# Expert stage: w1 loaded twice with its sums a block ahead, casts queued behind bank copies, first half-pass of w2 by plain products

## The chip, the core and the metric

The kernel runs on one core of a Trainium2 chip. The metric is the device time of one execution in microseconds (us), the median over runs. TensorE (PE) multiplies, VectorE (DVE) and ScalarE (ACT) copy, add and cast, GpSimd (POOL) does elementwise differences, and the DMAs are issued from SyncE's queue (SP).

## The reference, cut to what matters

```python
x = attention(q, k, v)                       # 2 x 8 heads, 576 tokens, 64 wide
x = (silu(x @ w_gate) * (x @ w_val)) @ w_out  # 1152 tokens, 512 wide, 1536 hidden
P = sinkhorn(exp(x @ w_gate2 - max))          # 1152 x 8, eight rounds of row and column scaling
for e in range(8):                            # the stage that is changed
    h = np.maximum(x @ w1[e], 0.0)            # 512 -> 1024
    out += P[:, e:e + 1] * (h @ w2[e])        # 1024 -> 512
```

## The kernel before

Every float32 operand is split into a high part (a rounding cast on ACT, `fp32r`) and a low part (the difference, `sub`, line 70, on DVE), and every product is three matmuls: high by high, high by low, low by high. Attention and the gated layer come first and are not changed; the expert stage (`experts`) starts at 378 us of the profile.

The expert stage goes through 16 passes, `n`: half of an expert's hidden units each (four tiles of 128). A pass has two halves of the tokens, `c`. For each half, `Group` computes the hidden units with w1: seven products `p1` to `p7` instead of eight (Strassen's scheme in Winograd's form), so w1 is needed both plain (`b`, 768 columns) and as differences of its 256-column blocks (`t`, 1024 columns). `Pair` multiplies four 128-token tiles of the first half by w2, again by seven products, so w2 is needed plain (`Q[:, 0:4]`) and as differences (`Q[:, 4:7]` and `T2`). The rest is done by plain products: `tile_product` (line 850), 12 matmuls of 512 columns a tile; in every pass that is the odd tile (`last_tile`) and the four tiles of the second half.

Units are interleaved by `block`: two Groups, or two Pairs, in the order p1, p5 of each, then p6, p2, then p7, p3, then p4. A product accumulates onto a bank that an ACT copy has seeded (`seeded`, line 689: it copies the running sum into a fresh PSUM bank and returns it, named `u`, `y` or `b`), so the next product on that bank waits for the copy. The last p4 of a block is done inside the next block (`late`). PE and POOL keep the written order; the order on ACT, DVE and SP is laid by the scheduler, which fills gaps by its own estimates. Within one engine instructions run strictly in that order.

The weights: `load_raw` (line 97) loads 512 KB of w1 or w2 into one of three buffers `raw`. `prep1` loads a w1 tile once, casts `b` from it (line 115), then lets POOL make the differences in place (`differences`, line 104, four operations on 128x256), then casts `t` from the same buffer (line 120). In every pass these steps stand at p1 of the first Pair. `second_sums` does the same for w2's differences: load, POOL, cast (line 865); `second` loads w2 again and casts it plain. The two w1 tiles and the two w2 tiles of a pass therefore give 16 POOL operations, one after the other, in the Pair block and the Group block behind it.

`behind()` queues what is traced inside it, on ACT, after the last bank copy (`mark[0]`). `emit` scales and adds a product to the output accumulator `acc` on DVE (line 780). `gate` computes P in 14 small steps, between products of the first passes, at the counts in `GSTEPS`.

Of the kernel before, what the change touches and what calls it, by code (L numbers as in the profile page):

```python
# [29 lines left out]
GSTEPS = {10, 16, 45, 54, 58, 78, 83, 88, 107, 112, 117}  # L30
# [30 lines left out]
def fused(ctx, tc, qk, v, rope, wgv, wo, wg2, w1, w2, out):  # L61
# [44 lines left out]
    def prep1(W1, n, u, src):  # L106

        if u not in W1:  # L110
            W1[u] = new_w(), new_w()
        raw = load_raw(src)
        yield
        (bh, bl), (th, tl) = W1[u]
        nc.scalar.copy(out=bh[:, 0:768], in_=raw[:, 0:768])
        sub(bl[:, 0:768], raw[:, 0:768], bh[:, 0:768])
        yield
        differences(raw, (1, 3, 0, 2))
        yield
        nc.scalar.copy(out=th, in_=raw)  # L120
        sub(tl, raw, th)
        yield
# [488 lines left out]
    def w_out(x2, x32, ps, uh, ul, W1):  # L611
# [12 lines left out]
        for d in range(KD):  # L624
            for c in range(NC):
                if d == KD - 1 and c == 0:
                    for _ in prep1(W1, 0, 0, w1[0, :, 0:WU]):
                        pass
# [15 lines left out]
    def experts(x, x32, ep, banks, W1):  # L644
# [22 lines left out]
        def sums(c):  # L667
            s = token_sums(x32, c)
            o = token_halves(c)[2]
            for i in (1, 2, 0, 3):  # L670
                nc.scalar.copy(out=sh[:, i, :, o], in_=s[i])
                sub(sl[:, i, :, o], s[i], sh[:, i, :, o])
# [19 lines left out]
        mark = [None]  # L692
# [77 lines left out]
        def emit(n, t, half, src, w=256):  # L770
            dst = acc[:, t, 256 * half:256 * half + w]
            e = n // 2
            if e == 0:
                if (t, half) not in touched:
                    touched.add((t, half))
# [88 lines left out]
        def cast(hi, lo, src):  # L864
            nc.scalar.copy(out=hi, in_=src)  # L865
            sub(lo, src, hi)

# [51 lines left out]
        def second_sums(n, u):  # L919
            raw = load_raw(source(w2, n, u))  # L920
            yield
            differences(raw, (0, 1, 2, 3))
            yield
            cast(*(y[:, 4:7, u] for y in Q), raw[:, 0:768].rearrange("p (a c) -> p a c", a=3))
            cast(*(y[:, u] for y in T2), raw[:, 768:1024])
            yield

        def second(n, u):
            raw = load_raw(source(w2, n, u))
            yield  # L930
            cast(*(y[:, 0:4, u] for y in Q), raw.rearrange("p (a c) -> p a c", a=4))
            yield
# [102 lines left out]
        def steps(make, n):  # L1035

            if n >= NV:
                return lambda: None
            gens = [make(n, u) for u in range(2)]
            return lambda: [next(y, None) for y in gens]  # L1040

        def first_(n, u):
            return prep1(W1, n, u, source(w1, n, u))

        acc = None
        with tc.manual_schedule(engines={mybir.EngineType.PE, mybir.EngineType.Pool}):
            A, C = Group(0, 0, 0), Group(0, 0, 1)
            A.p1()
            for _ in range(3):
                next(g)  # L1050
            with behind():
                sums(0)
            A.p2()
            C.p1(True)
            for _ in first_(0, 1):
                pass
            step2, step1 = steps(second_sums, 0), steps(second, 0)
            step2()
            step2()
            A.p6()  # L1060
            with behind():
                step2()
# [3 lines left out]
            A.p3()  # L1066
            acc = ep.tile([128, NTT, DM], F32, tag="acc", name="acc")
            Bq = Group(0, 1, 0)
            Bq.p1()
            with behind():  # L1070
                sums(1)
# [3 lines left out]
            step1()  # L1075
            Bq.p2()
            Bq.p7()
            Bq.p3()
            C.again()
            Bq.p4()  # L1080
            for t in token_tasks(0):
                run(t)
            tokens_left(0, 0)

            def held(step):
                def go():
                    with behind():
                        step()
# [106 lines left out]
```

## Time and profile before

| | before |
|---|---|
| median of 3 runs | 1163.57 us (1162.12 to 1164.08) |
| profiled execution, its own time | 1161.39 us |
| its span | 1159.6 us |
| PE busy | 1130.0 us (97%) |
| DVE busy | 858.9 us (74%) |
| ACT busy | 635.8 us (55%) |
| POOL busy | 355.2 us (31%) |
| mean DMA rate | 84 GB/s |

The span is the profile's own clock from its first to its last instruction; the execution's time lies 1.8 us above it. A busy share is an average over the whole span: attention, the gated layer, and the 16 passes of the expert stage, which fill the last two thirds.

### The profile page before, as it was taken

The page shows a single profiled execution, that of the slowest core. Times are in us where ns is not written, and L with a number is a line of the kernel's source. Part 1 is how long each engine was busy: PE and PEld are TensorE (multiplying, and loading weights), DVE is VectorE, ACT ScalarE, POOL GpSimd, SP SyncE. Part 2 cuts the span into 40 slices and gives each one's busy share as a digit, 9 for nine tenths or more (in the row PEclk, how much of TensorE's full clock was granted, in tenths as well). Part 3 has the DMA queues.
Part 4 walks back from the last instruction along what each step waited for, and adds up shares of the span by engine and source line. Part 5 has one row for each costly group of instructions (what it writes and reads, how often), then busy time and mean ns, then how long its engine had stood idle before and what let it go on. Part 6 is the DMA issues. An engine that isn't in the chain of part 4 may idle for free.

```text
span 1159.6 us, 19384 instructions
## 1 busy us (share of the span) xinstructions
PE 1130.0 (97%) x7431; PEld 1042.0 (90%) x7431; DVE 858.9 (74%) x1498; ACT 635.8 (55%) x1323; POOL 355.2 (31%) x360
## 2 busy tenths in 40 slices
PE   9999999999999899999999999999999999999998
PEld 7777789999999788898998989989899898998997
DVE  6777879988752877887767877768677786777864
ACT  4777744444332776465654656546565465564651
POOL 5777210000010450432504415144051350523500
PEclk9999999999999999999999999999999999999999
DMA  5877413322221131211312122122221222212202
GB/s 179 243 204 192 150 40 112 119 88 79 75 68 43 55 107 40 73 56 56 94 52 73 56 71 94 37 73 71 65 85 37 74 73 74 73 38 73 82 11 82
DMA packets 29837, 97.57 MB, mean 84 GB/s; under 512 B 4912, under 2 KB 5424, under 8 KB 28336
## 3 DMA queue, kind: packets, MB, share of 16 engines
q1 hardware_dynamic: 29744, 96.34, 27.1%
q8 instruction: 58, 0.95, 0.3%
q14 instruction: 35, 0.29, 0.1%
HBM read 81.58 MB, written 2.36 MB: 72 GB/s over the span
## 4 chain that ended last, share of the span: by engine, by line
PE 71%; POOL 20%; DVE 5%; issue 3%; ACT 2%; POOLq 0%; DVEq 0%; ACTq 0%
POOL raw L104 20%; PE y L850 19%; PE u L174 5%; PE u L176 4%; PE u L175 4%; PE s L299 4%; PE pv L411 4%; PE t L339 3%; PE po L176 2%; PE po L175 2%; PE po L174 2%; PE pg L174 2%; PE pv L176 2%; PE pg L176 2%; PE pv L174 2%
## 5 line engine op out<-in xcount | busy, mean ns | idle before, releaser
L104 POOL TENSOR_TENSOR raw<-raw 128x256 f32<-128x256 f32 x256 | 263.7, 1037 | 686.0 <-DVE wl L70 639.4
L70 DVE TENSOR_TENSOR hl<-d,hh 128x256 fp32r<-128x256 f32 (+1 forms) x224 | 138.5, 630 | 49.3 <-ACT hh L865 49.2
L865 ACT CAST hh<-d 128x256 fp32r<-128x256 f32 (+1 forms) x224 | 115.0, 527 | 91.5 <-PE y L850 45.1
L174 PE MATMUL u<-sh,wh 128*128 128x288 f32 x384 | 115.2, 300 | 10.8 <-ACT u L689 10.8
L175 PE MATMUL u<-sl,wh 128*128 128x288 f32 x384 | 113.4, 295 | 0.7 <-DVE sl L70 0.7
L176 PE MATMUL u<-sh,wl 128*128 128x288 f32 x384 | 113.3, 295 | 0.0
L70 DVE TENSOR_TENSOR wl<-raw,wh 128x768 fp32r<-128x768 f32 (+1 forms) x64 | 78.6, 1229 | 31.2 <-ACT wh L120 31.2
L850 PE MATMUL y<-qh,hl 128*128 128x512 f32 x256 | 99.7, 389 | 0.0
L850 PE MATMUL y<-qh,hh 128*128 128x512 f32 x256 | 99.6, 389 | 0.0
L850 PE MATMUL y<-ql,hh 128*128 128x512 f32 x256 | 99.6, 389 | 0.0
L699 DVE TENSOR_TENSOR d<-u,d 128x288 f32<-128x288 f32 x128 | 58.0, 456 | 42.2 <-PE u L176 41.2
L174 PEld LDWEIGHTS u<-sh,wh 128*128 128x128 f32 x384 | 72.6, 189 | 14.8 <-ACT u L689 14.8
L70 DVE TENSOR_TENSOR ql<-raw,qh 128x768 fp32r<-128x768 f32 (+1 forms) x64 | 71.9, 1123 | 16.1 <-ACT qh L865 16.0
L780 DVE SCALAR_TENSOR_TENSOR acc<-y,Pm,acc 128x512 f32<-128x512 f32 (+1 forms) x98 | 65.7, 670 | 23.8 <-PE y L850 21.6
L174 PE MATMUL c<-xh,wh 128*128 128x288 f32 x256 | 75.5, 295 | 0.3 <-ACT d L944 0.3
L176 PE MATMUL c<-xh,wl 128*128 128x288 f32 x256 | 75.2, 294 | 0.0
L175 PE MATMUL c<-xl,wh 128*128 128x288 f32 x256 | 75.0, 293 | 0.0
L175 PEld LDWEIGHTS u<-sl,wh 128*128 128x128 f32 x384 | 72.7, 189 | 0.9 <-DVE sl L70 0.9
L176 PEld LDWEIGHTS u<-sh,wl 128*128 128x128 f32 x384 | 72.7, 189 | 0.0
L886 DVE TENSOR_TENSOR d<-d 128x256 f32<-128x256 f32 x128 | 53.4, 419 | 18.2 <-ACT d L702 17.6
L865 ACT CAST qh<-raw 128x768 fp32r<-128x768 f32 (+1 forms) x64 | 60.2, 942 | 7.5 <-POOL raw L104 7.5
L320 ACT ACTIVATE p<-s,ng 128x576 f32<-128x576 f32 x64 | 47.6, 745 | 28.9 <-DVE ng L304 28.4
(225 smaller groups left out, 3439.1 us busy)
## 6 DMA issues: line engine op xcount, KB each, us to landing
raw<-in_w SPq DMA_DIRECT2D x96, 512.0 KB, 3.9
raw<-in_wgv SPq DMA_DIRECT2D x11, 1024.0 KB, 4.9
x<-in_qk SPq DMA_DIRECT2D x14, 576.0 KB, 5.6
raw<-in_wo SPq DMA_DIRECT2D x12, 512.0 KB, 3.7
x<-hl SPq DMA_DIRECT2D x42, 144.0 KB, 3.5
x<-hl SPq DMA_DIRECT2D x14, 288.0 KB, 3.6
v<-in_v SPq DMA_DIRECT2D x8, 320.0 KB, 4.5
out<-acc SPq DMA_DIRECT2D x9, 256.0 KB, 2.0
```

The source lines that it names most:

```text
L70: (eng or nc.vector).tensor_tensor(out=out_, in0=a, in1=hi.bitcast(F32), op=ALU.subtract)
L104: nc.gpsimd.tensor_tensor(out=o, in0=p, in1=q, op=ALU.subtract)
L174: nc.tensor.matmul(ps, wh[wsl], xh[xsl], start=first, stop=False, skip_group_check=onto)
L175: nc.tensor.matmul(ps, wh[wsl], xl[xsl], start=False, stop=False, skip_group_check=onto)
L176: nc.tensor.matmul(ps, wl[wsl], xh[xsl], start=False, stop=last, skip_group_check=onto)
L299: nc.tensor.matmul(ps[:, c, o:o + ks.stop - ks.start], q, k, start=t == 0, stop=t == len(terms) - 1)
L320: nc.scalar.activation(out=pr.rearrange("p (a c) -> p a c", a=2), in_=SC.pop((n, u))[:, :, 0:288], func=AF.Exp, bias=R.pop((n, u)), scale= ...
L699: nc.vector.tensor_tensor(out=out_, in0=a, in1=b, op=ALU.add)
L780: nc.vector.scalar_tensor_tensor(out=dst, in0=src, scalar=Pm[:, t, e:e + 1], in1=dst, op0=ALU.mult, op1=ALU.add)
L850: nc.tensor.matmul(po.rearrange("p (a c) -> p a c", a=2), a, b, start=m == j == 0, stop=m == 3 and j == 2)
L865: nc.scalar.copy(out=hi, in_=src)
L886: nc.vector.tensor_tensor(out=o, in0=a, in1=b, op=op)
```

## The change

- w1 is loaded twice: 768 columns into `R[2]` for the plain cast (`b_load`, `b_cast`), 1024 into `R[0]` or `R[1]` for the differences (`t_load`, `t_cast`). The three buffers are fixed ones now. `t_load` stands in the Group block of the second half, right after the plain w2 cast that frees the buffer, a block ahead of its cast; w2's differences (`s_load`) follow the w1 cast in the Pair block, and are cast in the Group block behind it.
- The casts stand behind the last bank copy on ACT and, on DVE, behind the last addition (`mark[1]`).
- In pass 0 the four tiles of the first half are done by `plain_tile` instead of two Pairs, so pass 0 needs no differences of w2; the first sums of x are made before the first product; `GSTEPS` has other counts.

```diff
-        raw = load_raw(src)
...
-        nc.scalar.copy(out=bh[:, 0:768], in_=raw[:, 0:768])
-        sub(bl[:, 0:768], raw[:, 0:768], bh[:, 0:768])
...
-        differences(raw, (1, 3, 0, 2))
...
-        nc.scalar.copy(out=th, in_=raw)
-        sub(tl, raw, th)
+    def cast(hi, lo, src):
+        nc.scalar.copy(out=hi, in_=src)
+        sub(lo, src, hi)
...
+                    nc.sync.dma_start(out=R[2][:, 0:768], in_=w1[0, :, 0:768])
+                    nc.sync.dma_start(out=R[0], in_=w1[0, :, 0:WU])
+                    cast(*(y[:, 0:768] for y in W1[0][0]), R[2][:, 0:768])
+                    differences(R[0], (1, 3, 0, 2))
...
         def behind():
-            return tc.issue_after(mark[0].ins)
+            with ExitStack() as st:
+                for m in mark:
+                    if m is not None:
+                        st.enter_context(tc.issue_after(m.ins))
+                yield
         def add(out_, a, b):
-            nc.vector.tensor_tensor(out=out_, in0=a, in1=b, op=ALU.add)
+            mark[1] = nc.vector.tensor_tensor(out=out_, in0=a, in1=b, op=ALU.add)
...
+        def b_load(n, u):
+            load(2, w1, n, u, 768)
+        def b_cast(u):
+            cast(*(y[:, 0:768] for y in W1[u][0]), R[2][:, 0:768])
+        def t_load(n, u):
+            load(u, w1, n, u)
+            differences(R[u], (1, 3, 0, 2))
+        def t_cast(u):
+            cast(*W1[u][1], R[u])
+        def s_load(n, u):
+            load(u, w2, n, u)
+            differences(R[u], (0, 1, 2, 3))
+        def s_cast(u):
+            cast(*(y[:, 4:7, u] for y in Q), R[u][:, 0:768].rearrange("p (a c) -> p a c", a=3))
+            cast(*(y[:, u] for y in T2), R[u][:, 768:1024])
+        def q_cast(u, r):
+            cast(*(y[:, 0:4, u] for y in Q), R[r].rearrange("p (a c) -> p a c", a=4))
...
-                block([Pair(w, 0, s) for s in range(2)], merge(plain_tasks(w), {(1, 0): [held(step) if n == 1 else step, step, step]}),
+                if n == 1:
+                    for i in range(2):
+                        for r in range(2):
+                            plain_tile(0, 0, i, r)
...
+                else:
+                    block([Pair(w, 0, s) for s in range(2)], merge(plain_tasks(w), {
+                        (5, 1): [held(b_cast, 1), now(b_load, n + 1, 0)],
+                        (6, 0): [held(t_cast, 0), now(s_load, n, 0)],
+                        (2, 1): [held(t_cast, 1), now(s_load, n, 1)]} if n < NV else {}),
...
-                    block([Group(n, u, 0) for u in range(2)], {(6, 0): [step2]}, behind=BEHIND[1:])
+                    block([Group(n, u, 0) for u in range(2)], {(7, 1): [held(s_cast, 0), now(load, 0, w2, n, 0)]}, behind=BEHIND[1:])
                 last_tile(w)
...
+                    held(s_cast, 1)()
+                    load(1, w2, n, 1)
...
-                    block([Group(n, u, 1) for u in range(2)], {(6, 0): [step]}, behind=BEHIND[1:])
+                    block([Group(n, u, 1) for u in range(2)], {
+                        (1, 0): [held(q_cast, 0, 0)] + [now(t_load, n + 1, 0)] * (not last),
+                        (1, 1): [held(q_cast, 1, 1)] + [now(t_load, n + 1, 1)] * (not last),
+                        (3, 0): [held(b_cast, 0), now(b_load, n + 1, 1)] * (not last)}, behind=BEHIND[1:])
```

The order of ACT in the Pair block of one pass, before (`wh` is w1's high part, `raw` its buffer, `qh` and `xh<-raw` w2's differences, `hh` a cast of hidden units, `y`, `b`, `u2` the bank copies; every pass from the third on repeats it):

```order
L865 CAST hh0_4310<-d_4309 128x2x2x128 [waits PE_49,Activation_49]
L689 COPY y_11144<-x_11137 128x256 [waits PE_49]
L120 CAST wh_4152<-raw_11031 128x1024 [waits Pool_49]
L865 CAST hh1_4312<-d_4309 128x2x2x128 [waits PE_49]
L689 COPY b_11163<-y_11101 128x256 [waits PE_49]
L689 COPY b_11178<-y_11144 128x256 [waits PE_49]
L120 CAST wh_4387<-raw_11033 128x1024 [waits Pool_49]
L865 CAST xh_2317<-raw_11219 128x256 [waits DMAHW0_49,Pool_49]
L689 COPY u2_11230<-c11_11223 128x288 [waits DVE_49,PE_49]
```

And the same place of the changed kernel:

```order
L107 CAST hh0_4315<-d_4314 128x2x2x128 [waits PE_49,Activation_49]
L683 COPY y_11477<-x_11470 128x256 [waits PE_49]
L107 CAST wh_4157<-raw2_4152 128x768 [waits DMAHW3_49]
L107 CAST hh1_4317<-d_4314 128x2x2x128 [waits PE_49]
L683 COPY b_11498<-y_11450 128x256 [waits PE_49]
L107 CAST wh_4155<-raw0_4150 128x1024 [waits DMAHW1_49,Pool_49]
L683 COPY b_11520<-y_11477 128x256 [waits PE_49]
L107 CAST wh_4159<-raw1_4151 128x1024 [waits DMAHW2_49,Pool_49]
L683 COPY u2_11575<-c11_11568 128x288 [waits DVE_49,PE_49]
```

A plain cast of w1 from the third buffer has come in behind the second `y` copy, each 1024-column cast stands behind a `b` copy, and the cast of w2's differences no longer stands ahead of `u2`.

The order of DVE at the same place, before (`wl` is w1's low part, `acc<-b` the addition that reads bank `b`):

```order
L780 SCALAR_TENSOR_TENSOR acc<-z,Pm,acc 128x256 [waits PE_49]
L780 SCALAR_TENSOR_TENSOR acc<-z,Pm,acc 128x256
L70 TENSOR_TENSOR wl<-raw,wh 128x1024 [waits Activation_49]
L780 SCALAR_TENSOR_TENSOR acc<-x,Pm,acc 128x256 [waits PE_49]
L70 TENSOR_TENSOR hl_4313<-d,hh_4312 128x2x2x128 [waits Activation_49]
L780 SCALAR_TENSOR_TENSOR acc<-x,Pm,acc 128x256 [waits PE_49]
L780 SCALAR_TENSOR_TENSOR acc<-b,Pm,acc 128x256 [waits DVE_49,PE_49]
L70 TENSOR_TENSOR wl<-raw,wh 128x1024 [waits Activation_49]
L780 SCALAR_TENSOR_TENSOR acc<-y,Pm,acc 128x256 [waits PE_49]
L780 SCALAR_TENSOR_TENSOR acc<-b,Pm,acc 128x256 [waits DVE_49,PE_49]
```

And now:

```order
L779 SCALAR_TENSOR_TENSOR acc<-z,Pm,acc 128x256 [waits PE_49]
L779 SCALAR_TENSOR_TENSOR acc<-z,Pm,acc 128x256
L70 TENSOR_TENSOR wl<-raw_4152,wh 128x768 [waits DMAHW3_49,Activation_49]
L70 TENSOR_TENSOR hl_4318<-d,hh_4317 128x2x2x128 [waits Activation_49]
L779 SCALAR_TENSOR_TENSOR acc<-x,Pm,acc 128x256 [waits PE_49]
L70 TENSOR_TENSOR wl<-raw_4150,wh 128x1024 [waits DMAHW1_49,Activation_49]
L779 SCALAR_TENSOR_TENSOR acc<-x,Pm,acc 128x256 [waits PE_49]
L779 SCALAR_TENSOR_TENSOR acc<-b,Pm,acc 128x256 [waits DVE_49,PE_49]
L70 TENSOR_TENSOR wl<-raw_4151,wh 128x1024 [waits DMAHW2_49,Activation_49]
L779 SCALAR_TENSOR_TENSOR acc<-y,Pm,acc 128x256 [waits PE_49]
L779 SCALAR_TENSOR_TENSOR acc<-b,Pm,acc 128x256 [waits DVE_49,PE_49]
```

The two 1024-column differences keep their places among the additions, and one of 768 columns comes in ahead of them.

SP's queue for one pass of the changed kernel (before, it was six loads of 128x1024):

```order
L916 DMA raw_4152<-in_w 128x768 [waits DMAHW4_49,DVE_49]
L916 DMA raw_4152<-in_w 128x768 [waits DMAHW3_49,DVE_49]
L916 DMA raw_4150<-in_w 128x1024 [waits DMAHW1_49,DVE_49]
L916 DMA raw_4151<-in_w 128x1024 [waits DMAHW2_49,DVE_49]
L916 DMA raw_4150<-in_w 128x1024 [waits DMAHW5_49,DVE_49,Pool_49]
L916 DMA raw_4151<-in_w 128x1024 [waits DMAHW6_49,DVE_49,Activation_49]
L916 DMA raw_4150<-in_w 128x1024 [waits DMAHW7_49,DVE_49]
L916 DMA raw_4151<-in_w 128x1024 [waits DMAHW0_49,DVE_49]
```

In their order: the plain w1 of tile 1 and of the next pass's tile 0, w2 for its differences (two), w2 plain (two), the next pass's w1 for its differences (two). Each waits for the DVE difference that reads the buffer last.

## Rows read from the trace of the kernel before

**Rows 1.** The page: busy time, share of the span and instructions of each engine.

```profile
PE 1130.0 (97%) x7431; PEld 1042.0 (90%) x7431; DVE 858.9 (74%) x1498; ACT 635.8 (55%) x1323; POOL 355.2 (31%) x360
```

**Rows 2.** PE's waits, 500 to 1110 us: total, times, longest.

```profile
PE u L174 <- ACT u L689: 8.3, 13, 0.6
PE b L798 <- DVE acc L780: 5.7, 13, 0.4
```

**Rows 3.** PE's timeline in one pass: start, duration, instruction, idle before it.

```profile
566.86 0.28 PE L798 MATMUL b<-qh,hh 128*128 128x256 f32 x1
...
568.30 0.29 PE L174 MATMUL c<-xh,wh 128*128 128x288 f32 x1
...
569.79 0.29 PE L174 MATMUL p<-sh,wh 128*128 128x288 f32 x1
...
571.18 0.38 PE L798 MATMUL b<-qh,hh 128*128 128x256 f32 x1 [0.43 <-DVE acc L780]
...
574.39 0.29 PE L174 MATMUL c<-xh,wh 128*128 128x288 f32 x1
...
575.97 0.40 PE L174 MATMUL u<-sh,wh 128*128 128x288 f32 x1 [0.62 <-ACT u L689]
```

**Rows 4.** ACT's timeline in the same pass.

```profile
561.89 0.36 ACT L689 COPY y<-x 128x256 f32<-128x256 f32 x1 [0.16 <-PE x L798]
...
567.78 1.05 ACT L120 CAST wh<-raw 128x1024 fp32r<-128x1024 f32 x1 [2.24 <-POOL raw L104]
...
575.21 0.41 ACT L865 CAST xh<-raw 128x256 fp32r<-128x256 f32 x1 [1.21 <-POOL raw L104]
575.52 0.39 ACT L689 COPY u<-c 128x288 f32<-128x288 f32 x1
```

**Rows 5.** DVE's timeline in the same pass.

```profile
557.83 0.95 DVE L70 TENSOR_TENSOR wl<-raw,wh 128x768 fp32r<-128x768 f32 x1
...
568.86 1.48 DVE L70 TENSOR_TENSOR wl<-raw,wh 128x1024 fp32r<-128x1024 f32 x1 [0.93 <-ACT wh L120]
...
570.66 0.47 DVE L780 SCALAR_TENSOR_TENSOR acc<-b,Pm,acc 128x256 f32<-128x256 f32 x1
```

**Rows 6.** POOL's timeline in two passes, and all its differences (min/median/max ns).

```profile
511.22 17.42 POOL L104 TENSOR_TENSOR raw<-raw 128x256 f32<-128x256 f32 x16 [32.82 <-DVE wl L70]
558.91 17.40 POOL L104 TENSOR_TENSOR raw<-raw 128x256 f32<-128x256 f32 x16 [30.27 <-DVE wl L70]
...
L104 POOL TENSOR_TENSOR raw<-raw x249: 724/1052/1607, 379.0 to 1099.9; 128x256 f32<-128x256 f32 x125
```

**Rows 7.** The weights' loads of 512 KB, from issue to landing.

```profile
DMA to landing us min/median/max: 3.7/3.9/4.8
```

**Rows 8.** ACT's groups by form: the casts of hidden units and of 768 columns.

```profile
L865 ACT CAST hh<-d 128x512 fp32r<-128x512 f32 x128 | 78.9, 618 | 12.5 <-PE y L850 4.1 <-PE b L798 3.8 <-PE z L798 3.7
...
L115 ACT CAST wh<-raw 128x768 fp32r<-128x768 f32 x32 | 26.6, 834 | 14.0 <-PE u L175 12.2 <-issue 1.1 <-DMA raw<-in_w 0.7
```

**Rows 9.** DVE's groups by form: the differences of 1024 columns.

```profile
L70 DVE TENSOR_TENSOR wl<-raw,wh 128x1024 fp32r<-128x1024 f32 x32 | 47.8, 1493 | 31.2 <-ACT wh L120 31.2
...
L70 DVE TENSOR_TENSOR ql<-raw,qh 128x1024 fp32r<-128x1024 f32 x32 | 39.1, 1221 | 7.1 <-ACT qh L865 7.0
```

**Rows 10.** PE's waits, 380 to 435 us (pass 0).

```profile
PE u L174 <- DVE d L699: 1.9, 2, 1.2
PE p L174 <- ACT d L747: 1.0, 1, 1.0
...
PE u L175 <- DVE sl L70: 0.7, 1, 0.7
PE p L175 <- DVE sl L70: 0.6, 1, 0.6
```

**Rows 11.** PE's waits, 435 to 500 us (passes 1 and 2).

```profile
PE u L174 <- ACT u L689: 1.8, 1, 1.8
PE pc L975 <- DVE Pm L972: 0.9, 2, 0.5
```

**Rows 12.** The chain that ended last: four plain tiles of one pass.

```profile
537.77 10.89 PE y L850 x48
```

More of the change, by code (lines that the diff above doesn't have):

```diff
@@ L669, in sums, with split @@
             o = token_halves(c)[2]
-            for i in (1, 2, 0, 3):
-                nc.scalar.copy(out=sh[:, i, :, o], in_=s[i])
-                sub(sl[:, i, :, o], s[i], sh[:, i, :, o])
+            def split(*which):
+                for i in which:
+                    cast(sh[:, i, :, o], sl[:, i, :, o], s[i])
+            return split
         def operand(i, c):
@@ L774, in emit @@
                 if (t, half) not in touched:
-                    touched.add((t, half))
+                    touched.update((t, h) for h in range(half, half + w // 256))
                     nc.scalar.copy(out=dst, in_=src)
@@ L917, in tokens_left, with load @@
                 cast(left[0][:, u, :, dst], left[1][:, u, :, dst], v[:, index(n, c, u), :, src])
[L919 to L932, printed above, removed]
+        def load(i, w, n, u, k=WU):
+            if n < NV:
+                nc.sync.dma_start(out=R[i][:, 0:k], in_=source(w, n, u)[:, 0:k])
+        def b_load(n, u):
[15 more added lines that the diff above has]
+            cast(*(y[:, 0:4, u] for y in Q), R[r].rearrange("p (a c) -> p a c", a=4))
         def gate():
@@ L1047, in experts @@
             A, C = Group(0, 0, 0), Group(0, 0, 1)
+            sums(0)(1, 2, 0, 3)
+            t_cast(0)
             A.p1()
+            b_load(0, 1)
             for _ in range(3):
                 next(g)
-            with behind():
-                sums(0)
             A.p2()
             C.p1(True)
[L1055 to L1059, printed above, removed]
+            b_cast(1)
+            load(0, w2, 0, 0)
+            load(2, w2, 0, 1)
+            t_load(0, 1)
+            split = sums(1)
             A.p6()
             with behind():
-                step2()
+                t_cast(1)
+            t_load(1, 1)
             C.p2()
@@ L1078, in experts, with held @@
             Bq.p3()
+            with behind():
+                q_cast(1, 2)
+            b_load(1, 0)
             C.again()
             Bq.p4()
-            for t in token_tasks(0):
-                run(t)
+            for half in range(2):
+                tokens = [Tokens(0, half, i) for i in range(2)]
+                if half == 0:
+                    for y in tokens:
+                        y.plain()
+                        y.rest()
             tokens_left(0, 0)
-            def held(step):
+            def held(f, *args):
```

70 lines of the change are left out of this document (31 added, 39 removed).

## The prediction

> **What bounds the kernel now.** I read the page's busy times first. PE is busy 97% of the span [rows 1], so nothing that other engines do can be worth more than PE's gaps, and what PE itself gets to do more is paid in full. The second view is PE's waits. From 500 to 1110 us, thirteen passes, there are only two kinds, each once a pass: a product onto a bank `u` waits for ACT's bank copy, and a product onto `b` waits for DVE's addition that still reads that bank [rows 2]. POOL starts its sixteen differences every 47.69 us (511.22 and 558.91), which is the length of a pass [rows 6].
>
> The wait column understates what a gap costs, since the first matmul behind it is longer too (0.38 us where 0.28 is usual). So I take the gaps from starts on PE's timeline [rows 3]. Two products of six 256-column matmuls take 568.30 - 566.86 = 1.44 us, 0.72 each; a w1 product (288 columns) and one of these take 569.79 - 568.30 = 1.49, so a w1 product takes 0.77. The product that starts at 569.79 would end its turn at 570.56, the next starts at 571.18: 0.62 lost. The one at 574.39 would end at 575.16, the next starts at 575.97: 0.81 lost. That is 1.4 us a pass.
>
> What ends these gaps is read on the engines behind. The `u` copy starts at 575.52, directly behind a cast of w2's differences for which ACT had stood 1.21 us, waiting for POOL [rows 4]. The addition that frees `b` runs at 570.66, behind the 1.48 us difference of w1 that DVE began at 568.86, for which it waited on the cast, which had waited 2.24 us for POOL [rows 4, 5]. Both waits of PE are therefore one cause: sixteen POOL differences in a row, 17.4 us from 558.91 to 576.31 [rows 6], with casts ahead of bank copies in ACT's strict order.
>
> **The change part by part: the two gaps.** POOL's work stays sixteen operations a pass, but w1's eight are made a block earlier. I follow ACT's new order on the old clock. The cast `wh` from the third buffer needs the reload, which waits for the difference that ends at 557.83 + 0.95 = 558.78 [rows 5]; a load of 512 KB lands 3.9 us after its issue [rows 7], and I take that for 384 KB too: 562.7. ACT is through with the second `y` copy at 562.25 [rows 4], so it stands 0.45 us. Then the cast (0.83), a cast of hidden units (0.62) [rows 8] and the first `b` copy (0.36, as the `y` copy) end at 564.5. PE wants it two products before 566.86, at 565.4: slack 0.9. The 1024-column cast (1.05) and the second `b` copy end at 565.9, wanted at 566.86; the second cast ends at 567.0. POOL is in neither step.
>
> On DVE the first 1024-column difference then begins near 565.6 and the second near 568.0, with two additions between. Such a difference takes 1.49 us for w1, beside POOL's work, and 1.22 for plain w2, when POOL is idle [rows 9]; POOL will be idle here, so I take 1.22, and 1.49 as the bound. Two more additions (0.47) free `b` at 569.9 (570.4 at the bound), and PE wants it at 570.56. The first gap closes, by a hair at the bound. For the second, the `u` copy now has nothing of POOL's ahead of it and comes right after its product. Both gaps gone is 13 x 1.4 = **18.2 us**.
>
> **Where the stalls go.** w2's differences: the loads go out when the two w1 differences are done (566.8 and 569.2), the first lands at 570.7, and eight POOL operations at the median 1.05 us [rows 6] end at 579.1. ACT comes to their second cast near 577 and stands there 1 to 2 us. Behind it stand three relus and then casts of hidden units into tiles that the odd plain tile still reads. The four plain tiles began at 537.77 [rows 12], in this pass at 585.46, or 584.1 without the two gaps; the odd tile ends a w1 product earlier, at 583.3. So the stall has 4 us of cover; without it each us costs 14 us in all.
>
> w1's differences: the second half's Groups begin when the four tiles end, 537.77 + 10.89 + 47.69 - 1.4 = 594.95. Two bank copies, two casts of w2 (1.05 each), a copy of 0.64 and a cast of 0.62 stand in a row on ACT, new there; they end the second w2 cast near 599.9. The next bank copy would be done at 600.9 by durations alone; ACT starts overlap by 0.1 (575.21 + 0.41 against 575.52, [rows 4]), so about 600.2, and PE wants it eight products after 594.95, at 601.1. The loads land at 602.4 and 605.0, POOL is through at 610.8, and the second cast is wanted at 565.9 + 46.3 = 612.2: slack 1.4.
>
> The extra loads are 32 x 384 KB; they cost nothing as long as the reload is on time, as above. In SP's order each load waits for the one ahead, but the releases come in the same order.
>
> **The start.** In pass 0 PE lost 4.2 us in five waits for the first sums of x, for an addition queued behind w2's differences, and for a copy that stood behind a cast [rows 10]; with 0.17 more each (0.62 against the 0.43 shown), 5.0. The sums now come ahead of the first product, and w2's differences and their casts are gone from this pass. Bounds: nothing comes back, or 5.0; I take 4.2, since the earlier sums alone clear 1.3 and the missing casts clear the others. The 1.8 us wait of pass 2 [rows 11] is the POOL wait in another size, 2.0 with the longer matmul. The plain tiles cost: four take 10.89 us [rows 12], two Pairs fourteen products of 0.72, 10.1, so 0.8 is lost. The gate's waits for `Pm` (0.9, [rows 11]) lie on DVE and I leave them; other counts could move them by 1 us either way.
>
> Sum: 18.2 + 2.0 + 4.2 - 0.8 = 23.6. The profiled execution, 1161.4 us, becomes 1137.8; the median lies 2.2 above that execution, so it becomes **1140.0**.
>
> **A rule against it.** POOL's differences take from 0.72 to 1.61 us [rows 6], and DVE's two-input differences 1.22 or 1.49 with POOL idle or busy [rows 9]: the two slow each other. The Trainium skill, "SBUF — State Buffer", section "SBUF: two separate sides", says that GpSimd and a VectorE instruction with two SBUF inputs lock a shared port pair, and the loser waits for the whole instruction; the trace agrees, since 0.72 + 0.95 is 1.67. By that rule the median is no price for a moved operation, which leads to the first rival.
>
> **Rivals.** *POOL late again.* If w1's eight differences meet DVE's casts more often in their new place, at 1.61 us each they end at 602.4 + 12.9 = 615.3, 3.1 us late; less the 0.65 us that DVE has in hand, 2.45 a pass comes back, 32 us: 1172. The point from which it costs is 1.31 us an operation. At 1.45 they end at 614.0, 1.15 a pass comes back, 15 us, and the time is 1155; that is the case I give a chance to. For it: the range of durations. Against: the same mix of DVE work lay beside POOL before, and gave 1.05.
>
> *Half.* One of the two gaps stays, by a queue place that I have mis-walked, or a bank copy behind the two new w2 casts comes 0.6 us late: 8 us come back, 1148.
>
> *The reload.* The cast in the Pair block waits for a load that can't be issued before the first tile's difference, and both `b` copies, both big casts and the `u` copy stand behind it on ACT. Each us that it lands later than 562.7 + 0.9 goes to PE, fourteen times; at the worst landing seen, 4.8 [rows 7], nothing is lost. It takes back everything from 1.7 us beyond that, a landing of 6.5 us, and at 7.0 the kernel is 7 us slower: 1171. Only a load held back by its queue could do that.
>
> *No change*: the waits move to other bank copies and PE loses as much there, 1163.5.
>
> **Chances.** About 0.2% is what can be told from no change. Forecast 0.74 (1136 to 1144 by its bounds: below, the start's whole 5.0, the gate's 0.9 and up to 1.6 of smaller waits of these stretches that the rows leave out; above, nothing back at the start); half 0.10; POOL late, but faster still, 0.06; no change 0.03; the reload, or another cast that stands ahead of a bank copy, 0.07. That is faster 0.89, same 0.03, slower 0.08. The range 1135 to 1150 takes in the forecast and the half.
>
> **What would show it.** Right: PE's two waits from 500 us are gone, a pass takes 46.3 us, POOL works in two stretches of eight, the 1024-column casts wait for nothing, the cast of w2's second differences shows a wait on POOL that PE doesn't see. Wrong: a wait of PE's `b` product on ACT's copy (the reload), casts of `wh` that wait for POOL (rival one), or new waits of `u` in the second half's Groups.

## The result, and the profile after

| | before | after |
|---|---|---|
| median | 1163.55 us (1162.12 to 1164.08, 4 runs) | 1131.17 us (1131.08 to 1132.23, 4 runs) |
| profiled execution, its own time | 1161.39 us | 1131.08 us |
| its span | 1159.6 us | 1129.2 us |

The ratio is 0.9726 (95% interval 0.9709 to 0.9743). The kernel gained 32.4 us where 23.6 was forecast, and the time lies below the range of 1135 to 1150.

The page's busy times after, against [rows 1]:

```profile
PE 1120.2 (99%) x7395; PEld 1040.0 (92%) x7395; DVE 822.2 (73%) x1476; ACT 640.5 (57%) x1305; POOL 301.1 (27%) x352
```

From 500 to 1110 us the view of PE's waits is empty: both rows of [rows 2] are gone. The rows of 377 to 500 us, against [rows 10, 11] (`pc` and `Pm` belong to the gate):

```profile
PE u L160 <- ACT u L683: 1.0, 3, 0.4
PE pc L983 <- DVE Pm L980: 0.2, 1, 0.2
```

POOL's timeline, against [rows 6]: two stretches of eight. The median of an operation falls from 1.05 to 0.74 us; by the stretches, sixteen operations took 17.4 us and take 14.4, 1.09 and 0.90 each. The first stretch is w1's (the casts `wh` follow it), the second is that of w2.

```profile
546.37 7.46 POOL L104 TENSOR_TENSOR raw<-raw 128x256 f32<-128x256 f32 x8 [24.41 <-DMA raw<-in_w]
560.96 6.92 POOL L104 TENSOR_TENSOR raw<-raw 128x256 f32<-128x256 f32 x8 [7.13 <-DMA raw<-in_w]
...
L104 POOL TENSOR_TENSOR raw<-raw x208: 731/742/2174, 500.6 to 1072.4; 128x256 f32<-128x256 f32 x104
```

ACT's timeline at the place of [rows 4]: the casts stand behind the `b` copies, the reload is waited for 0.22 us, and nothing of POOL's stands ahead of `u`.

```profile
552.21 0.36 ACT L683 COPY y<-x 128x256 f32<-128x256 f32 x1
552.78 0.84 ACT L107 CAST wh<-raw 128x768 fp32r<-128x768 f32 x1 [0.22 <-DMA raw<-in_w]
553.53 0.61 ACT L107 CAST hh<-d 128x512 fp32r<-128x512 f32 x1
554.04 0.36 ACT L683 COPY b<-y 128x256 f32<-128x256 f32 x1
554.35 1.05 ACT L107 CAST wh<-raw 128x1024 fp32r<-128x1024 f32 x1
555.30 0.36 ACT L683 COPY b<-y 128x256 f32<-128x256 f32 x1
555.60 1.04 ACT L107 CAST wh<-raw 128x1024 fp32r<-128x1024 f32 x1
559.43 0.38 ACT L683 COPY u<-c 128x288 f32<-128x288 f32 x1 [2.79 <-PE c L162]
```

DVE at the place of [rows 5]: the second difference of 1024 columns follows at once and takes 1.21 us, so the addition behind it, and the one that frees `b`, are not held up.

```profile
557.72 1.21 DVE L70 TENSOR_TENSOR wl<-raw,wh 128x1024 fp32r<-128x1024 f32 x1
558.85 0.47 DVE L779 SCALAR_TENSOR_TENSOR acc<-y,Pm,acc 128x256 f32<-128x256 f32 x1
559.25 0.47 DVE L779 SCALAR_TENSOR_TENSOR acc<-b,Pm,acc 128x256 f32<-128x256 f32 x1
```

The budget is made from the chains: in each kernel the four plain tiles of [rows 12] mark a pass. Two such sets, thirteen passes apart, before:

```profile
490.08 10.89 PE y L850 x48
...
1110.04 10.91 PE y L850 x48
```

and the same two after:

```profile
482.17 10.89 PE y L849 x48
...
1079.20 10.89 PE y L849 x48
```

| stretch | before | after | gained | forecast |
|---|---|---|---|---|
| to the first product of the expert stage | 377.96 | 378.56 | -0.6 | 0 |
| from there to the first of the two sets | 112.12 | 103.61 | 8.5 | 5.4 |
| thirteen passes | 619.96 | 597.03 | 22.9 | 18.2 |
| the end | 49.6 | 50.0 | -0.4 | 0 |
| median over the profiled execution | 2.2 | 0.1 | 2.1 | 0 |

A pass took 47.69 us and takes 45.92: 1.77 less, where 1.4 was forecast.

### The profile page after: what moved, and what is told of

The parts are those of the page before. It is cut to its first block, busy times and chain, and to the rows that moved or that the text cites. A ratio compares the mean times of both kernels' runs of the same rounds, so it can differ in the third digit from the quotient of the medians.

```text
span 1129.2 us, 19336 instructions
## 1 busy us (share of the span) xinstructions
PE 1120.2 (99%) x7395; PEld 1040.0 (92%) x7395; DVE 822.2 (73%) x1476; ACT 640.5 (57%) x1305; POOL 301.1 (27%) x352
## 4 chain that ended last, share of the span: by engine, by line
PE 96%; DVE 2%; ACT 1%; issue 0%; POOL 0%; ACTq 0%; DVEq 0%; POOLq 0%
PE y L849 20%; PE u L160 6%; PE u L162 6%; PE u L161 6%; PE s L285 4%; PE pv L397 4%; PE b L797 4%; PE y L797 4%; PE x L797 4%; PE t L325 3%; PE c L160 3%; PE c L162 3%; PE c L161 3%; PE po L162 2%; PE po L161 2%; PE po L160 2%
## 5 line engine op out<-in xcount | busy, mean ns | idle before, releaser
L104 POOL TENSOR_TENSOR raw<-raw 128x256 f32<-128x256 f32 x248 | 209.6, 850 | 711.7 <-DMA raw<-in_w 672.5
L70 DVE TENSOR_TENSOR hl<-d,hh 128x256 fp32r<-128x256 f32 (+1 forms) x218 | 133.8, 620 | 37.6 <-ACT hh L107 33.1
L849 PE MATMUL y<-qh,hh 128*128 128x512 f32 x272 | 106.1, 390 | 0.0
L849 PE MATMUL y<-qh,hl 128*128 128x512 f32 x272 | 106.0, 390 | 0.0
L849 PE MATMUL y<-ql,hh 128*128 128x512 f32 x272 | 105.9, 389 | 0.0
L70 DVE TENSOR_TENSOR wl<-raw,wh 128x768 fp32r<-128x768 f32 (+1 forms) x64 | 74.8, 1168 | 10.4 <-ACT wh L107 9.9
L107 ACT CAST wh<-raw 128x768 fp32r<-128x768 f32 (+1 forms) x64 | 60.2, 941 | 27.2 <-PE u L161 16.6
L70 DVE TENSOR_TENSOR ql<-raw,qh 128x1024 fp32r<-128x1024 f32 (+1 forms) x62 | 67.8, 1093 | 9.6 <-ACT qh L107 7.8
L306 ACT ACTIVATE p<-s,ng 128x576 f32<-128x576 f32 x64 | 47.7, 745 | 29.7 <-DVE ng L290 29.3
L849 PEld LDWEIGHTS y<-qh,hl 128*128 128x128 f32 x272 | 51.0, 188 | 10.7
```

The source lines that it names most:

```text
L70: (eng or nc.vector).tensor_tensor(out=out_, in0=a, in1=hi.bitcast(F32), op=ALU.subtract)
L104: nc.gpsimd.tensor_tensor(out=o, in0=p, in1=q, op=ALU.subtract)
L306: nc.scalar.activation(out=pr.rearrange("p (a c) -> p a c", a=2), in_=SC.pop((n, u))[:, :, 0:288], func=AF.Exp, bias=R.pop((n, u)), scale= ...
L849: nc.tensor.matmul(po.rearrange("p (a c) -> p a c", a=2), a, b, start=m == j == 0, stop=m == 3 and j == 2)
```

## The experiments

The theory was the prediction's: both gaps of a pass come from POOL, whose sixteen differences in a row make casts late, and the change closes them by making w1's differences a block earlier from a second load. The first rival that grew out of the trace after: the place of the casts in the strict queues of ACT and DVE does it, and POOL's timing nothing.

### Taking the queueing away, and taking the second load away

*No queueing.* The changed kernel with its loads and its earlier differences, but the casts of the passes lie where the scheduler puts them.

```diff
             def held(f, *args):
                 def go():
-                    with behind():
-                        f(*args)
+                    f(*args)
```

> The changed kernel with the casts of the passes no longer queued behind the bank copies; w1 is still loaded twice. Theory: both parts are needed. In ACT's new order the second big cast of w1 stands ahead of the second y copy, which PE wants about 1 us before POOL is through with that buffer (553.8 us in the changed kernel's pass), so 1 to 2 us a pass come back: 1144 to 1157 us, and PE waits again for ACT's bank copies. Rival, the second load alone takes POOL off the path: 1131 to 1135 us, no new wait of PE above 0.2 us.

1160.83 us (1159.53 to 1162.39), ratio 0.9983 (0.9974 to 0.9993). Nearly the whole gain is gone, more than either expectation held. A pass takes 47.7 us, as before the change. PE's waits from 500 us, and ACT's timeline in one pass:

```profile
PE u L160 <- ACT u L683: 8.9, 13, 0.7
PE y L797 <- ACT y L683: 7.8, 13, 0.8
...
560.85 1.05 ACT L107 CAST wh<-raw 128x1024 fp32r<-128x1024 f32 x1 [0.87 <-POOL raw L104]
...
562.29 0.83 ACT L107 CAST wh<-raw 128x768 fp32r<-128x768 f32 x1
563.02 0.37 ACT L683 COPY y<-x 128x256 f32<-128x256 f32 x1
...
571.59 0.41 ACT L107 CAST xh<-raw 128x256 fp32r<-128x256 f32 x1 [1.55 <-POOL raw L104]
```

Two gaps a pass are back, now behind ACT's copies `u` and `y`, with the casts ahead of them. Earlier differences alone shorten no pass.

*One load.* From the third pass on, w1 is loaded once, a block ahead, and POOL's differences stand between its two casts again: the first tile's four still in the block ahead, the second tile's four in the Pair block itself. The casts stay held.

```diff
+        def bt_cast(u):
+            cast(*(y[:, 0:768] for y in W1[u][0]), R[u][:, 0:768])
+            differences(R[u], (1, 3, 0, 2))
...
-                        (5, 1): [held(b_cast, 1), now(b_load, n + 1, 0)],
+                        (5, 1): [held(bt_cast, 1)],
```

> The changed kernel with one load of w1 from the third pass on: the plain cast reads the buffer first, then POOL makes the differences in it, then the big cast, all queued as in the changed kernel. Theory, both parts are needed: POOL stands between two casts again, the second big cast comes about 3 us later than now (four operations of 0.74 us behind the second plain cast), DVE and ACT have 2 to 2.5 us in hand there, so 0 to 1 us a pass comes back: 1131 to 1144 us, with a wait of the casts on POOL in every pass. Rival, the second load is what closes the gaps: both gaps return, 1.77 us a pass, 1154 us or more. Other rival, the queueing alone does it: 1131 to 1132 us.

1131.22 us (1129.74 to 1131.64), ratio 0.973 (0.9715 to 0.9744): the changed kernel's time. ACT's waits from 500 us show the late differences, and PE shows no wait in that stretch:

```profile
ACT wh L107 <- POOL raw L104: 50.3, 13, 3.9
```

ACT stands 3.9 us a pass for POOL, more than the 2.24 of [rows 4], and PE loses nothing: both `b` copies are done before the late cast, and the `u` copy behind it is still in time. The second load is worth nothing.

*Which queue.* `behind()` names two marks. With ACT's alone, and with DVE's alone:

```diff
-                for m in mark:
+                for m in mark[:1]:
```

```diff
-                for m in mark:
+                for m in mark[1:]:
```

> The changed kernel, but a held cast is queued behind the last bank copy on ACT alone; on DVE its difference lies where the scheduler's own estimates put it. If ACT's order is what counts (with no holding at all, PE waited 0.7 to 0.8 us twice a pass for ACT's copies and for nothing of DVE's), nearly all the gain stays: 1131 to 1136 us. If DVE's order carries half of it, as the old waits of the b product on DVE's addition would suggest, 7 to 11 us come back: 1138 to 1143. PE's waits from 500 us on tell the two apart: none, or b and x products on DVE.

> The changed kernel, but a held difference is queued behind the last addition on DVE alone; the cast itself lies on ACT where the scheduler puts it. If ACT's order is what counts, the waits of PE on ACT's u and y copies return, 1.5 to 1.8 us a pass, and the time is 1154 to 1161. If the two orders share the gain, 1142 to 1148. If DVE's order is what counts, 1131 to 1136.

ACT's mark alone gives 1131.12 us (ratio 0.9728, 0.9711 to 0.9744), DVE's alone 1158.25 (0.9964, 0.9952 to 0.9975), with PE waiting on ACT's copies again:

```profile
PE y L797 <- ACT y L683: 8.9, 13, 1.5
PE u L160 <- ACT u L683: 6.0, 12, 0.5
```

In the changed kernel ACT's mark is enough, and DVE's adds nothing to it. DVE's mark is the last `add`, and the additions to the accumulator in these passes (`emit`) are not among those, which is likely why it moves little.

### Queueing alone, on the kernel before

The kernel before, with its single load and POOL's sixteen in a row. First `behind()` and `add` are those of the changed kernel, with both marks, all casts are held, and w1's second casts are traced behind the first p6 of the Pair block:

```diff
-                block([Pair(w, 0, s) for s in range(2)], merge(plain_tasks(w), {(1, 0): [held(step) if n == 1 else step, step, step]}),
+                block([Pair(w, 0, s) for s in range(2)], merge(plain_tasks(w), {(1, 0): [held(step), step], (6, 0): [held(step)]}),
...
-                    step2()
+                    held(step2)()
...
-                    step1()
+                    held(step1)()
```

> The kernel before, with its single load of w1 and POOL's sixteen differences in a row, and with the casts held behind the last bank copy and the last addition; the casts of w1's differences are also traced behind the first p6 of the Pair block instead of its first p1. If the place in the queues is what closes the gaps, the passes give back 17 to 23 us and the start little: 1139 to 1146. If the differences' place on POOL matters, as the prediction held, casts still stand up to 2 us for POOL ahead of bank copies and less than a third comes back: 1156 to 1163.

1155.61 us, ratio 0.9941 (0.9924 to 0.9958), between the two expectations. A pass takes 47.17 us. Both old gaps are gone and a new wait is there: the `p` product waits for w1's difference, 1.0 us a pass, since the held plain cast starts POOL 3.1 us later against the plain tiles (24.2 us behind them, where it was 21.1). POOL then is late in every pass.

```profile
PE p L176 <- DVE wl L70: 12.8, 13, 1.0
```

So the plain casts were set free again from the third pass on:

```diff
-{(1, 0): [held(step), step], (6, 0): [held(step)]}
+{(1, 0): [held(step) if n == 1 else step, step], (6, 0): [held(step)]}
```

> As the held kernel before, but the plain casts of w1 are not held (from pass 2 on), so that POOL begins its sixteen differences where it did before. Holding all of them had put POOL's start 3.1 us later against the four plain tiles, and PE then waited 1.0 us a pass for the late half of w1's differences. If the place of the casts in the queues is enough, and POOL's sixteen in a row are harmless when they begin on time, the passes take 45.9 to 46.2 us and the time is 1139 to 1144. If w1's differences must be made a block earlier, a wait of the p product on DVE stays, and the time is 1150 to 1158.

1149.14 us, ratio 0.9881 (0.9867 to 0.9896), a miss of both expectations: a pass takes 46.77 us. The `u` gap is gone and the `b` gap stays. POOL begins 21.1 us behind the plain tiles, as in the kernel before; its sixteen take 16.64 us instead of 17.40, but that is not what freed `u`: the casts of w2's differences now stand behind the `u` copies, and the one that was late (569.94 here, 575.52 in [rows 4]) comes 2.5 us earlier against the tiles and waits for PE alone. PE's waits from 500 us, POOL's row, that copy, and DVE's timeline:

```profile
PE b L803 <- DVE acc L785: 7.7, 13, 0.6
...
555.86 16.64 POOL L104 TENSOR_TENSOR raw<-raw 128x256 f32<-128x256 f32 x16 [30.15 <-DVE wl L70]
...
569.94 0.38 ACT L689 COPY u<-c 128x288 f32<-128x288 f32 x1 [0.19 <-PE c L176]
...
565.82 1.47 DVE L70 TENSOR_TENSOR wl<-raw,wh 128x1024 fp32r<-128x1024 f32 x1 [1.75 <-ACT wh L120]
567.21 0.47 DVE L785 SCALAR_TENSOR_TENSOR acc<-y,Pm,acc 128x256 f32<-128x256 f32 x1
567.61 0.47 DVE L785 SCALAR_TENSOR_TENSOR acc<-b,Pm,acc 128x256 f32<-128x256 f32 x1
```

DVE stands 1.75 us for the cast, which waits 2.7 us for POOL, and the addition that frees `b` is behind. Two theories were left: POOL must be earlier, or the difference must stand behind that addition. The next kernel changes DVE's order alone, ACT's order in a pass being the same: the additions of `emit` become the mark, and w1's second difference comes two additions later. With it w2's held differences come one to three instructions later; in neither kernel does one of them stand in the Pair block ahead of the addition that frees `b`.

```diff
-                nc.vector.scalar_tensor_tensor(out=dst, in0=src, scalar=Pm[:, t, e:e + 1], in1=dst,
+                mark[1] = nc.vector.scalar_tensor_tensor(out=dst, in0=src, scalar=Pm[:, t, e:e + 1], in1=dst,
...
-(6, 0): [held(step)]}
+(6, 0): [held(step, 0)], (7, 1): [held(step, 1)]}
```

> The kernel before with its casts held, as in the version whose pass took 46.77 us, and with the second 1024-column difference of w1 on DVE queued behind the last addition of the accumulator, so that it stands two additions later; ACT's order and POOL's sixteen differences in a row are unchanged. If that place is what holds back the addition that frees b, the wait of PE's b product goes and a pass takes 45.9 us: 11 us less than that version, 1137 to 1140. If POOL being late is what costs, a wait of the same size appears at another product and the time stays at 1147 to 1150.

1135.85 us, ratio 0.9783 (0.9763 to 0.9803), a little below the 1137 expected. A pass takes 45.91 us, as expected, PE shows no wait from 500 us, and POOL still works sixteen in a row, with ACT standing for it:

```profile
ACT wh L120 <- POOL raw L104: 34.9, 13, 2.7
...
553.66 16.74 POOL L104 TENSOR_TENSOR raw<-raw 128x256 f32<-128x256 f32 x16 [28.93 <-DVE wl L70]
...
561.79 0.47 DVE L785 SCALAR_TENSOR_TENSOR acc<-y,Pm,acc 128x256 f32<-128x256 f32 x1
562.36 0.48 DVE L785 SCALAR_TENSOR_TENSOR acc<-b,Pm,acc 128x256 f32<-128x256 f32 x1
563.61 1.47 DVE L70 TENSOR_TENSOR wl<-raw,wh 128x1024 fp32r<-128x1024 f32 x1 [0.77 <-ACT wh L120]
```

That settles the passes: the places close both gaps, and POOL's timing need not be better than it was (3.1 us later, in the version with all casts held, it did cost).

*All but the loads.* The same with pass 0's plain products, the new gate counts and pass 0's casts held:

```diff
-            for t in token_tasks(0):
-                run(t)
+            for y in (Tokens(0, 0, i) for i in range(2)):
+                y.plain()
+                y.rest()
...
+                if n == 1:
+                    tokens = [Tokens(0, 1, i) for i in range(2)]
+                    for i in range(2):
+                        for r in range(2):
+                            plain_tile(0, 0, i, r)
...
+            with behind():
+                step1(0)
```

> The same, with pass 0's plain products, the new gate counts and pass 0's casts held behind bank copies as in the changed kernel: all of the change except the second load of w1, its differences made a block ahead, and the sums ahead of the first product. If those three are worth nothing, the time is the changed kernel's: 1130 to 1133. If the earlier differences are worth something in the passes, 1137 or more.

1128.49 us (1127.94 to 1128.82), ratio 0.9708 (0.9694 to 0.9723): it is below what was expected, and 2.7 us below the changed kernel, with no overlap of the two ranges of runs. The two were timed at different times, and the intervals of their ratios to the kernel before overlap (0.9694 to 0.9723, 0.9709 to 0.9743); the profiled spans, 1126.8 and 1129.2, differ as the times do. PE's waits are empty from 377 us to the end of the passes. From the first expert product to the first marked set of tiles it takes 101.78 us, 1.8 less than the changed kernel, whose three `u` waits of that stretch are gone too. It moves 96.5 MB where the changed kernel moves 109.1.

### Sizes of single terms

*Plain tiles.* Passes 4, 6, 8 and 10 do their first half by plain products too.

```diff
+        EXTRA = {4, 6, 8, 10}
...
-                if n == 1:
+                if n == 1 or w in EXTRA:
```

> The changed kernel with four more passes (4, 6, 8 and 10) that do the first half's four tiles by plain products instead of two Pairs, as pass 0 does; their differences of w2 are still made, and not used. Prediction's term: 10.89 against 10.08 us, 0.8 us a pass, so 3.2 us: 1134.4 us, and those passes 46.7 us long instead of 45.92. Rival, plain tiles also save waits, since DVE and ACT have fewer sums to make: less than 1 us in all, 1131 to 1132 us.

1134.38 us: 3.2 more than the changed kernel, 0.8 each, as forecast. In its trace such a pass takes 46.90 us against 45.92, which is 1.0 each; the stretch ahead of the passes came out 0.5 us shorter. The price lies between 0.8 and 1.0.

*Pass 0 alone*, the plain products and the gate counts put into the kernel before, without w2's differences in that pass:

```diff
-GSTEPS = {10, 16, 45, 54, 58, 78, 83, 88, 107, 112, 117}
+GSTEPS = {10, 16, 46, 55, 62, 68, 74, 80, 87, 109, 114}
...
+                            plain_tile(0, 0, i, r)
```

> The kernel before with pass 0's first half by plain tiles and the gate's new counts alone: no differences of w2 in pass 0, w1 loaded once, no queueing in the later passes, sums of x as before. Between the first product of the expert stage and the plain tiles of pass 2 the change gained 8.5 us, of which about 2.7 lie in pass 2's own gaps. Theory: most of the other 5.8 us come from the missing differences of w2: 4 us, 1159.5 us; the waits for the first sums (1.3 us and 0.2 more) stay. Rival, the gains of pass 0 come from the earlier sums and the queueing: less than 1 us, 1163 us.

1162.68 us, ratio 0.9999 (0.999 to 1.0009): no gain in time. PE's waits of 377 to 500 us sum to 5.8 us where they were 8.5, but they lie elsewhere, and two of some 2 us are new:

```profile
PE c L174 <- ACT acc L776: 2.2, 1, 2.2
PE pc L975 <- DVE Pm L972: 1.9, 1, 1.9
```

Behind the first of these the granted clock was 0.50 from 424 to 428 us of the profiled execution, while the kernel before's shows 1.00 throughout. The mean clock of its ten executions was 0.995 to 0.999, and the two at 0.999 took 1161.0 us, where the kernel before took 1161.65 to 1162.0 at 0.999 at the same time. So the run doesn't show that the missing differences are worth nothing: some of what they gave was lost to the clock (last section).

*The first sums*, behind the first product again, and *the second plain w2 cast of pass 0*, moved behind the tokens' sums:

```diff
-            sums(0)(1, 2, 0, 3)
...
+            with behind():
+                sums(0)(1, 2, 0, 3)
```

```diff
-            with behind():
-                q_cast(1, 2)
-            b_load(1, 0)
...
+            with behind():
+                q_cast(1, 2)
+            b_load(1, 0)
```

> The changed kernel, with the first sums of x behind the first product, as before. The prediction gave the earlier sums 1.3 us (two waits of PE for them in pass 0); with the longer matmul behind each wait 1.5 to 1.7: 1132.5 to 1133. If DVE has time for them anyway, 1131.

> The changed kernel, with the second plain w2 cast of pass 0 moved behind the tokens' sums, since PE waits there twice for ACT in pass 0 (1.0 us in all). If this cast is what stands ahead of the u copies, 0.6 to 1.0 us are gained: 1130.2 to 1130.6. If not, 1131.

1130.88 us and 1130.72 (ratios 0.973, 0.9713 to 0.9746, and 0.9726, 0.9712 to 0.9741): the same as the changed kernel, with the same waits of PE. The earlier sums are worth nothing; the kernel with pass 0 alone changed has no wait for `sl` either, with the sums where they were.

*The reload late*, issued twice in thirteen passes:

```diff
             load(2, w1, n, u, 768)
+            if n > 2 and u == 1:
+                load(2, w1, n, u, 768)
```

> The changed kernel; in thirteen passes the plain reload of w1 for the second tile is issued twice in a row into the same buffer, so that it lands about 3.2 us (one load) later. The cast of it stands on ACT ahead of both b copies. By the prediction's slack of 0.9 us, 2.3 us a pass are lost: 1161. In the changed kernel's trace the first b copy is done 1.34 us before its product starts: 1.9 a pass, 1156. If ACT's stand is hidden from PE, 1131. PE's new wait should be that of the first b product on ACT's b copy.

1136.49 us: 0.4 a pass more than the changed kernel, below both sums and above the 1131 of a hidden stand. ACT's order came out another way: the reload's cast now stands behind the first `b` copy and the first 1024-column cast, ACT stands 1.3 us a pass for it (16.7 in thirteen), and only the second `b` copy comes late. This run therefore doesn't measure the slack of 0.9, which was worked out for the other order.

*POOL doubled*, every difference of thirteen passes done twice:

```diff
+                nc.gpsimd.tensor_tensor(out=spare, in0=p, in1=q, op=ALU.subtract)
                 nc.gpsimd.tensor_tensor(out=o, in0=p, in1=q, op=ALU.subtract)
```

> The changed kernel, every POOL difference of thirteen passes done twice (once into a spare tile), so sixteen more operations a pass of 0.74 us each or more, 5.9 us more in each stretch of eight. By the prediction's threshold of 1.31 us an operation, from which each us goes to PE, 3.4 us a pass or more come back: 1175 or above. By the changed kernel's trace, POOL is through about 12 us before w1's casts are due, and the casts of w2's second differences have some 4 us of cover: 1131 to 1145. If lateness on POOL never mattered, 1131.

1167.14 us (1164.71 to 1174.22), 36 us or 2.8 a pass more than the changed kernel, which none of the three expectations held: POOL does become the bound once it is late enough for the product itself. Part of it is TensorE's clock (last section): its mean was 0.992 in the profiled execution, which took 1170.2 us, and 0.995 in those of 1165. The passes of its trace whose granted clock was 1.00 take 48.1 to 48.5 us, 2.2 to 2.5 more than the changed kernel's. The threshold of the prediction asked 3.4 or more, so it was set too low.

```profile
PE p L162 <- DVE wl L70: 15.4, 13, 1.3
PE p L160 <- ACT wh L107: 7.7, 12, 1.4
```

## Why the prediction was right and wrong

**What bounds the kernel, right.** PE's gaps were all there was to win. Both waits went, POOL works in two stretches of eight, and the 1024-column casts wait for POOL only 0.8 us in thirteen passes. The pass is shorter than forecast (45.92, not 46.3), and w2's second casts hardly stand for POOL (2.4 us in all thirteen passes, where 1 to 2 us each were expected). The plain tiles cost 0.8 to 1.0 us a pass, where the sum had 0.8.

**"Both waits of PE are therefore one cause: sixteen POOL differences in a row" failed.** The sentence went on "with casts ahead of bank copies in ACT's strict order", and that half was the cause. It was two places, one on each engine: w2's casts ahead of `u` on ACT (closed by holding, with POOL's sixteen in a row where they were), and w1's second difference ahead of the addition that frees `b` on DVE (closed by two places in the order, with POOL's sixteen there still). The step "POOL's work stays sixteen operations a pass, but w1's eight are made a block earlier" carried no time of its own: without the queueing it shortened no pass, and with the places right it was not needed. The changed kernel leaves the second difference at its early place on DVE, where only the earlier differences keep it from standing; the version with one load has it later and lets ACT stand 3.9 us. Either closes the gap. The walk along the queues was right; from it I concluded which engine was late, and never asked whether lateness or order was to be charged.

**The size of a gap, mis-sized.** Eighteen us became 22.9. The gaps of [rows 3] were taken from start to start, but the product behind a gap takes 0.1 us longer too, and that I left out; and a third, small gap stood at the first `b` product. In the kernel before:

```profile
565.13 0.28 PE L798 MATMUL x<-qh,hl 128*128 128x256 f32 x1
565.32 0.39 PE L798 MATMUL b<-qh,hh 128*128 128x256 f32 x1
...
571.18 0.38 PE L798 MATMUL b<-qh,hh 128*128 128x256 f32 x1 [0.43 <-DVE acc L780]
...
572.00 0.29 PE L174 MATMUL c<-xh,wh 128*128 128x288 f32 x1
...
575.97 0.40 PE L174 MATMUL u<-sh,wh 128*128 128x288 f32 x1 [0.62 <-ACT u L689]
...
576.87 0.30 PE L174 MATMUL c<-xh,wh 128*128 128x288 f32 x1
```

The `b` product takes 572.00 - 571.18 = 0.82 where 0.72 is usual, the `u` product 0.90 where the changed kernel's takes 0.80, and the first `b` product starts 0.19 behind a matmul whose turn is 0.12, and is itself 0.1 longer. So 1.43 + 0.1 + 0.1 + 0.17 is 1.8, and 1.77 was measured. Two readings of the prediction were slightly off and changed nothing: a w1 product takes 0.79 to 0.80 us by the starts, not 0.77, which takes 0.05 off the 1.43; and in the walk along DVE 568.0 is the start of the second difference at the bound of 1.49 us, not at 1.22.

**The start, mis-sized, and its reasons wrong.** 8.5 came back instead of 5.4 (2.0 + 4.2 - 0.8). From 377 to 500 us PE waited 8.5 us in all before; the forecast counted 6.0 of them and left out 2.5, and 1.2 are still there after, which is 1.3 more than forecast. The other 1.8 is of the size of what a gap costs beyond its wait: nine waits are gone, each with 0.17 by the prediction's figure (0.19 by its two numbers, 0.62 and 0.43), worked out there for five (0.85) and not taken, and with 0.1 for the longer product. No run takes it apart further. "The earlier sums alone clear 1.3" failed: they clear nothing that is not cleared without them. "The missing casts clear the others" was not borne out either: with pass 0 alone changed, two new waits of some 2 us stood in the place of the old ones, the clock fell behind one of them, and no time was gained. What the missing differences give by themselves stays open; with the casts queued as well and w1 loaded once, every wait there was gone.

**The median, a constant that was none.** I let the median stand 2.2 us above the profiled execution. That was 2.1 of the 32.4 (last section).

**The rivals.** POOL late again and the reload were not what happened, but POOL doubled shows that the first is real: 2.2 to 2.5 us a pass came back at the full clock. Its threshold, 1.31 us an operation, was not reached, since w1's eight took 7.46 us, 0.93 each. (The median of 0.74 says less: it is 0.745 in the version with POOL's sixteen in a row and the places right, whose stretch is as long as 16.7 us.) The rule that the prediction weighed (the Trainium skill, "SBUF — State Buffer", section "SBUF: two separate sides") agrees with that: w1's 1024-column differences went from 1493 to 1214 ns on the whole [rows 9], and from 1.49 to 1.21 us in the rows above. It bore on the durations; it did not decide the time.

## What to carry to other kernels

When a consumer waits for an engine that waits for another, ask two things apart: is the late result itself wanted, or does it only stand in a strict queue ahead of something that is? Only an experiment that changes one order and leaves the late engine late tells them apart, and the cheaper repair is the order: here holds behind the last bank copy and one difference two places later (others of w2 moved with it) gave in the passes what the change got with a second load and 12.6 MB more. The Trainium skill, "Perfetto Trace Analysis", section "Tensor Engine Instruction (MATMUL, LD_WEIGHTS)", calls ACT, DVE and GpSimd strict FIFOs; the two DVE timelines above, 46.77 against 45.91 us a pass by two places, show what that can cost. And count a gap from the start of the product ahead to the start of the product behind the next one.

## What the hardware showed that was not expected

A gap of PE of some 2 us was followed, in some executions and not in others, by a stretch at the lower of TensorE's two clock levels (1.2 instead of 2.4 GHz; the granted clock reads 0.50). Two versions of the kernel before, with all casts held (1155.61 us) and with the plain ones free (1149.14 us), show the same wait of 2.1 us at the same product. In the windows (start to end, length, PE busy, granted clock, DMA share, GB/s) of the first of them the clock falls behind it:

```profile
390.00:392.00 2.00, 0.03 (x1) 1.00 0.48 106
392.00:396.00 4.00, 4.00 (x24) 0.65 0.62 215
396.00:400.00 4.00, 4.00 (x18) 0.50 0.00 0
400.00:402.00 2.00, 2.00 (x16) 0.99 0.00 0
```

and in those of the second it doesn't:

```profile
390.00:392.00 2.00, 0.94 (x8) 1.00 0.10 12
392.00:396.00 4.00, 2.94 (x24) 1.00 0.67 215
396.00:400.00 4.00, 3.99 (x29) 1.00 0.12 47
```

The executions of the first that kept a mean clock of 1.0 took 1154.6 and 1154.7 us, those at 0.997 1156.5 and 1157.2: some 2 us. The kernel before is split alike: of 19 executions, 8 at 0.998 took 1163.5 to 1164.3 us and 11 at 0.999 or 1.0 took 1161.5 to 1162.5. The changed kernel's four were all at 1.0. That fits the 2.2 us by which the kernel before's median lay above its profiled execution: three of the four executions behind that median took 1163.5 to 1164.1, the times of the lower clock, though their clocks are not on record. So a part of what closing the gaps gave, 2.1 us, seems to lie in the clock and not in the gaps. Which gap of the kernel before it falls behind, no profile here shows, since the profiled execution kept its clock.
